# Queries of one chunk in a stage of their own instead of between attention's steps, and the order planned anew

## The chip, the cores and the metric

The kernel runs on one core of a Trainium2 chip. The core has engines that run their own instruction queues side by side: TensorE (PE in the profile; its weight loads are PEld), VectorE (DVE), ScalarE (ACT), GpSimd (POOL), and SyncE (SP), which here only issues DMA transfers. They meet through semaphores. SBUF is the on-chip memory, PSUM the eight banks that TensorE writes into.

The metric is the time of one execution on the device, in microseconds (us). Beside it there is a profiled execution, whose span is split up by engine, instruction and source line ("L640" is line 640 of the kernel before).

## The reference

Four blocks follow one another on x of 2048 tokens by 1024 features; each adds its result to x. Blocks 1 and 3 are a linear attention (A), blocks 2 and 4 softmax attention (B); A's and B's weights are used twice.

```python
def A(x, wqkv, w_phi, wo):
    q, k, v = ...                      # x @ wqkv, 32 heads of 32
    pq = q @ w_phi;  pk = k @ w_phi    # per head, 32 x 32
    phi_q = concat(softmax(pq), softmax(-pq))
    phi_k = concat(softmax(pk), softmax(-pk))
    kv = phi_k.T @ v;  z = sum(phi_k over tokens)
    o = (phi_q @ kv) / (phi_q @ z + 1e-6)
    return o @ wo

def B(x, wqkv, wo):
    q, k, v = ...
    p = softmax(q @ k.T * 32**-0.5)
    return (p @ v) @ wo

x = x + A(layernorm(x), ...);  x = x + B(layernorm(x), ...)
x = x + A(layernorm(x), ...);  x = x + B(layernorm(x), ...)
```

The text calls A the linear layer and B attention; so "the second linear layer" is the third block.

## The kernel before, in words

The tokens are four chunks (c = 0 to 3) of 512, each of four tiles of 128 rows. The features are eight groups (g) of 128, that is four heads each. x stays in SBUF (`xR`) for the whole kernel. All matrices are in bf16, sums in 32 bits.

**A linear layer** first makes keys and values of every chunk (`a_keys`), sums them up to a small state per head (`a_state`), and then makes, per chunk, the queries and with them the output (`a_queries`, `a_out`), the next row normalization (`ln_rows`), and the first keys and values for attention (`b_k`, `b_v`). For queries and keys the product of `wqkv` and `w_phi` is folded beforehand and lies in DRAM (`wd_q`, `wd_k`). `a_queries` treats half of a chunk's features at a time: four blocks of 128 features by 512 tokens, each made by eight matmuls (`mmg2`), then two exponentials on ScalarE (L1040), sums over heads, a weighting by the ratio of the two softmax sums, and numerator and denominator with the state.

**Attention** (`attention`) works through 32 turns, one for each chunk of queries and each group; a turn has 64 score blocks of 128 keys by 512 queries. A score block is one matmul (L1282). Two or three blocks lie in neighbouring PSUM banks and get one exponential on ScalarE (L1340). Other blocks are converted on VectorE instead (`convert`, L1438, one pass for a block; `exp_dve`, L1243 and L1248, four passes for a pair). Each block then goes into the products with values and with ones (L1481). Two sets of three PSUM banks hold scores, one bank the sums of L1481, and one bank, bank 7, is for "filling" work: the other keys, values and queries of attention, output projections of finished chunks, and, in the first attention, work of the second linear layer for chunks that are done. Filling work is made in 32-column form: four matmuls (L644) side by side for what elsewhere is one of 128 columns (L640). `mm` chooses the form.

In the first attention, when a chunk has its output, `ln_rows` normalizes it and `a_keys` makes its part of the keys' state (chunks 0, 1 and 2; the last chunk's follow in the linear layer's own stage). The normalized rows are kept in DRAM (`xd`, stored at L1719) and come back when queries are made (L1611).

For chunk 0 the kernel before goes a step further. `q_ahead` (L1011) loads chunk 0's rows again (L1724) and both halves of `wd_q` (L742), makes all eight blocks of queries in bank 7, copies each with VectorE to SBUF (L1022), and stores it to DRAM (`qf`, L1024). When the linear layer's stage begins, `a_queries` finds them in `q_saved`, loads them (L1036), and has no matmuls to do for them.

**What sets the order.** The kernel does not issue work in the order in which it is written. Every operation goes to a planner (`Sched`) with an engine, an expected duration, its predecessors, its buffers and a due time (`prio`); the planner plays through the engines' time and so fixes the order of each engine's queue, and where each buffer lies. Among its inputs are quotas on buffers of a kind (`QUOTA`; `MM_Q` is the number of PSUM banks that whole matmuls may hold, `MOST_E` that of exponentials waiting in attention), the due times of work (`PK` and `STEP`: row normalization and keys of chunks 0 to 2 in the first attention; `Q_LATE`: attention's queries of the late chunks; `OUT_AT`, `GO`, `PT`: output projections), and rules on when a score block goes to VectorE (`OPEN`, `NEAR`, `END`, `SLACK`). Where TensorE would have too little to do, the planner puts in filler matmuls whose results are not read (L1730 and L1734 with `onesD`, L1739 with `zero`).

The constant at the centre, and the two places that use it:

```python
QN = 1
...
            for c in range(QN, NC - 1):      # L1609: these chunks' rows come back for queries in the stage
                x_b, x_v = sb("xn", PO, C512)
...
            for c in range(QN):              # L1722: these chunks' queries are made in the first attention
                x_b, x_v = sb("xn1", PO, C512)
                q_ahead(c, at + QT[c], ...)
```

Of the kernel before, what the change touches and what calls it, by code (L numbers as in the profile page):

```python
# [61 lines left out]
class Sched:  # L62
# [139 lines left out]
    def run(self):  # L202
# [28 lines left out]
        while left:  # L231
# [173 lines left out]
RESERVE = 8 * 1024  # L405
LONG = {"kT", "v", "slab", "slabk", "xn", "xn1", "kvacc", "kvm", "zm", "wnat"}
MODEST = {"slabk", "xn1", "e1", "vp1", "pkf", "wo", "bo"}
MM_Q = 5
QUOTA = {"qf": 2, "qg": 6, "wqk": 1, "tl": 6, "pk": 6, "pv": 4, "kv": 3, "mm": MM_Q, "cmp": 3, "bc": 10, "num": 4, "wt": 4, "wx": 2, "fil": 5,
         "e": 6, "vp": 6, "e1": 4, "vp1": 4, "E": 10, "q2": 2, "kt": 4, "w2": 5, "oT": 26, "T": 4, "den": 2,  # L410
         "eq": 20, "ns": 12, "cw": 12, "hl": 6, "oc": 2, "slab": 8, "slabk": 3, "fin": 4,
# [10 lines left out]
QT = (184.5, 300, 310)  # L422
XQ = 5.39
QF_AT = 6.0
QN = 1
EVAC = (4, 4)
END = 28
FAR = (0, 0)
REST = 2.1
DIP = 4.0  # L430
# [19 lines left out]
HALF = (False, True)  # L450
VH = 3.38
V_LATE = (None, ((20.16, 6.58), (59.37, 7.17)))
Q_LATE = (lambda c, g: 104.52 + 4.56 * g if c == 2 else -5.67 + 18.61 * g, lambda c, g: 139.83 + 11.78 * g)
QL = (11, 9.91)
AW = 26
OUT_AT = (228.3, 245.85, 276.82)
GO = 2.98
BO = 296.78
PT = 3.56
QB = 18.16  # L460
PH = ((1, 22, 43), (1, 22, 43.51))
LA = 7.28
AHEAD_AT = 4
P0 = (133.6, 164.65, 226.59)
GAPS = (1.5, 2.78, 3.22)
PK = (142, 198.82, 255.37)
STEP = 3.45
AWAY = (-10, 12)
MIX = (lambda i: (1, 2, 1, 0)[i // 8], lambda i: (0, 0, 1, 0)[i // 8])
LOAD = (2.16, 2.38)  # L470
AHEAD = (25, 31)
SLACK = 4.16
THIRD_LOAD = (6.03, 1.29)
BOTH_LOAD = (0.97, 0.53)
EARLY = (80, 80)
# [3 lines left out]
XR = 40  # L479
SL = 30  # L480
HOLD = 0.81
OPEN = (0, 8)
MOST_E = (10, 15)
POOL = (0, 0)
BEHIND = (-3.39, 5.54)
NEAR = (10, 10)
LEAD = -1.02
MOST = (lambda i: 1 if i < 1 else 12, lambda i: 24 if i < 1 else 27)

# [18 lines left out]
def kernel(  # L508
# [746 lines left out]
    def attention(base, kT, vT, q_of, gate, most, mix, turns, pos, ahead, near, load, early, third_load, both_load, nb, opened, most_e, behind):  # L1255
# [114 lines left out]
        def lead():  # L1370
            return min(ahead, max(END, (len(units) - state["at"]) // 2))

# [11 lines left out]
        def wants(prio):  # L1384
# [4 lines left out]
            turn = pos[u[:2]]  # L1389
            if prio < prio_of(u) + SLACK:  # L1390
                return False
# [182 lines left out]
    for layer in range(2):  # L1574
# [31 lines left out]
        else:  # L1606
            wq_s = [slab("slab", second - SL + fc, wdq_v[:, :, fc * C512:(fc + 1) * C512], C512, [store["q"][fc]])
                    for fc in range(2)]
            for c in range(QN, NC - 1):  # L1609
                x_b, x_v = sb("xn", PO, C512)  # L1610
# [45 lines left out]
        for g in range(G):  # L1656
            pr = at + 10 * pos[(0, g)]
            w = slab("w2", pr - (QL[layer] + 3), B_w[:, :, g * P:(g + 1) * P], P) if g else wq0
            for qc in range(NC):
# [5 lines left out]
                else:  # L1665
                    pa = at + Q_LATE[layer](qc, g) if Q_LATE[layer](qc, g) is not None else pr + (AW if last else AWAY[qc - 2])
                    wa = w if pa < pr + 30 else slab("w2", pa - 3, B_w[:, :, g * P:(g + 1) * P], P)
# [6 lines left out]
        for qc, p0, gap in ((0, P0[0], GAPS[0]), (1, P0[1], GAPS[1]), (2, P0[2], GAPS[2])):  # L1674
            if last:
                p0, gap = OUT_AT[qc], GO
            for i in range(8):
# [13 lines left out]
        for i in range(G):  # L1691
            pr = p0 - 7 + PT * i
            t, fc = (i // 2, i % 2) if last else (i % 4, i // 4)
# [18 lines left out]
        if not last:  # L1712

            kv = new_kv()
            for c, p0 in ((0, PK[0]), (1, PK[1]), (2, PK[2])):
# [5 lines left out]
                    for i in range(4)]  # L1721
            for c in range(QN):  # L1722
                x_b, x_v = sb("xn1", PO, C512)
# [51 lines left out]
```

## Time and profile before

| | us |
|---|---|
| median of 3 runs | 2129.3 |
| lowest, highest | 2126.23, 2129.32 |
| profiled execution, its own time | 2128.77 |
| its span, first to last instruction | 2127.0 |
| first scores of the first attention start at | 309.4 |
| TensorE busy | 2074.9 |
| ScalarE busy | 1902.6 |
| VectorE busy | 1775.1 |

The span has five parts: loads and the first linear layer up to 309 us, the first attention up to about 1165, the second linear layer's stage up to about 1365, the second attention, and a short end. The rows are read as follows. A group has its line, engine and operation, what it writes and reads, how often it ran, then its busy time and the mean duration of one in ns, and last the idle time of the engine just before such instructions and what ended it. Durations of matmuls overlap, since they run in a pipeline: a matmul of 512 columns is listed with some 380 ns, while the next one starts after 0.22 us. A table by stretch gives, for the part of the span named first, its length and each engine's busy time in it, the granted TensorE clock as a share of full speed, the share of the DMA engines' time, and GB/s.

### The profile page before, as it was taken

The page shows a single profiled execution, that of the slowest core. Times are in us where ns is not written, and L with a number is a line of the kernel's source. Part 1 is how long each engine was busy: PE and PEld are TensorE (multiplying, and loading weights), DVE is VectorE, ACT ScalarE, POOL GpSimd, SP SyncE. Part 2 cuts the span into 40 slices and gives each one's busy share as a digit, 9 for nine tenths or more (in the row PEclk, how much of TensorE's full clock was granted, in tenths as well). Part 3 has the DMA queues.
Part 4 walks back from the last instruction along what each step waited for, and adds up shares of the span by engine and source line. Part 5 has one row for each costly group of instructions (what it writes and reads, how often), then busy time and mean ns, then how long its engine had stood idle before and what let it go on. Part 6 is the DMA issues. An engine that isn't in the chain of part 4 may idle for free.

```text
span 2127.0 us, 64995 instructions
## 1 busy us (share of the span) xinstructions
PE 2074.9 (98%) x27708; PEld 787.4 (37%) x27774; DVE 1775.1 (83%) x3310; ACT 1902.6 (89%) x2029; POOL 27.2 (1%) x83
## 2 busy tenths in 40 slices
PE   8999999999999999999999999999999999999999
PEld 5543443333333333333333434434333333333333
DVE  8866545757566899999999776798899999999998
ACT  7437769989999999999999577799999999999998
POOL 1000000000000000000000000000000000000000
PEclk9999999999999999999999999999999999999999
DMA  8730321121233322441355312211111122121111
GB/s 235 162 73 21 95 58 29 32 65 51 69 78 89 108 82 80 133 144 53 114 168 155 102 38 73 71 28 33 37 46 40 44 51 62 47 77 54 52 42 37
DMA packets 255467, 160.78 MB, mean 76 GB/s; under 512 B 147784, under 2 KB 229704, under 8 KB 255176
## 3 DMA queue, kind: packets, MB, share of 16 engines
q1 hardware_dynamic: 255176, 156.62, 27.2%
q8 instruction: 217, 3.56, 0.7%
q14 instruction: 74, 0.61, 0.1%
HBM read 89.72 MB, written 29.87 MB: 56 GB/s over the span
## 4 chain that ended last, share of the span: by engine, by line
PE 50%; ACT 26%; DVE 13%; issue 6%; DMA 4%; SPq 2%; ACTq 0%; DVEq 0%; POOL 0%; POOLq 0%
ACT arena L1340 23%; PE psum L640 15%; PE psum L644 13%; PE psum L1481 10%; PE psum L1282 9%; DVE arena L1438 4%; DVE work L1243 2%; DVE work L1248 2%; DVE arena L1248 2%; DMA arena<-rd 1%; PE psum L915 1%; DVE arena L1496 1%; SPq L731 1%; DMA arena<-in_A_wo_dram 1%; DMA arena<-arena 1%
## 5 line engine op out<-in xcount | busy, mean ns | idle before, releaser
L1340 ACT ACTIVATE arena<-psum 128x1536 bf16<-128x1536 f32 (+1 forms) x1332 | 1558.7, 1447 | 24.8 <-PE psum L1282 21.4
L644 PE MATMUL psum<-arena 128*32 128x512 bf16 (+1 forms) x9536 | 633.2, 365 | 9.2 <-DMA arena<-in_B_wqkv_dram 2.7
L1481 PE MATMUL psum<-arena 128*32 128x512 bf16 x4096 | 605.0, 383 | 1.3 <-DVE arena L1496 1.1
L1481 PE MATMUL psum<-arena,ones_bf 128*32 128x512 bf16 x4096 | 605.0, 383 | 0.0
L1282 PE MATMUL psum<-arena 32*128 32x512 bf16 x4096 | 523.9, 383 | 23.3 <-ACT arena L1340 16.5
L1438 DVE TENSOR_SCALAR arena<-psum 128x512 uint16<-128x512 f32 x663 | 446.4, 683 | 79.4 <-PE psum L1282 75.0
L640 PE MATMUL psum<-arena 128*128 128x512 bf16 (+1 forms) x1907 | 421.1, 372 | 7.8 <-issue 3.7
L1282 PEld LDWEIGHTS <-arena 32*128 32x128 bf16 x4096 | 160.0, 91 | 549.0 <-issue 545.5
L644 PEld LDWEIGHTS <-arena 128*32 128x32 bf16 x9536 | 209.1, 95 | 259.9 <-issue 162.2
L640 PEld LDWEIGHTS <-arena 128*128 128x128 bf16 x1968 | 185.7, 98 | 220.9 <-issue 21.4
L1243 DVE TENSOR_SCALAR work<-arena 128x1024 uint16<-128x1024 uint16 (+1 forms) x670 | 263.4, 415 | 2.3
L1481 PEld LDWEIGHTS <-arena 128*32 128x32 bf16 x4096 | 168.1, 95 | 211.8 <-issue 144.1
L1248 DVE TENSOR_TENSOR arena<-work 128x1024 bf16<-128x1024 bf16 x335 | 226.9, 677 | 2.6
L1248 DVE TENSOR_TENSOR work<-arena,work 128x1024 bf16<-128x1024 bf16 x335 | 226.5, 676 | 0.0
L1481 PEld LDWEIGHTS <-ones_bf 128*32 128x32 bf16 x4096 | 166.9, 95 | 22.3 <-issue 3.7
L880 ACT ACTIVATE arena<-psum 128x512 bf16<-128x512 f32 x80 | 43.7, 595 | 73.8 <-PE psum L640 67.8
L1145 DVE CAST arena<-psum 128x512 bf16<-128x512 f32 (+1 forms) x120 | 69.4, 579 | 42.7 <-PE psum L644 42.6
L1496 DVE COPY arena<-psum 128x512 f32<-128x512 f32 x126 | 86.0, 682 | 11.6 <-PE psum L1481 11.5
L884 DVE TENSOR_REDUCE arena<-arena 128x32 f32<-128x1024 bf16 x64 | 77.5, 1211 | 18.2 <-ACT arena L880 16.4
L1040 ACT ACTIVATE arena<-psum 128x512 bf16<-128x512 f32 x112 | 60.9, 616 | 25.7 <-PE psum L640 20.8
L893 DVE TENSOR_TENSOR arena<-psum,arena 128x1024 bf16<-128x1024 f32 x64 | 78.1, 1221 | 2.7
L685 ACT ACTIVATE arena<-xR 128x1024 bf16<-128x1024 bf16 x40 | 42.5, 1064 | 38.8 <-DVE xR L1119 38.8
(103 smaller groups left out, 994.1 us busy)
## 6 DMA issues: line engine op xcount, KB each, us to landing
arena<-in_B_wqkv_dram SPq DMA_DIRECT2D x66, 256.0 KB
arena<-rd SPq DMA_DIRECT2D x62, 256.0 KB
xa<-arena SPq DMA_DIRECT2D x48, 256.0 KB
arena<-in_A_wqkv_dram SPq DMA_DIRECT2D x40, 256.0 KB
arena<-in_B_wo_dram SPq DMA_DIRECT2D x40, 256.0 KB
arena<-arena SPq DMA_DIRECT2D x256, 32.0 KB
arena<-wd_k SPq DMA_DIRECT2D x32, 256.0 KB
arena<-arena SPq DMA_DIRECT2D x62, 128.0 KB
```

The costliest lines, as they stand in the source:

```text
L640: nc.tensor.matmul(out_, lhsT=lhsT, rhs=rhs, start=start, stop=stop, skip_group_check=True)
L644: nc.tensor.matmul(out_[ks, :], lhsT=lhsT[:, ks], rhs=rhs, start=start, stop=stop, tile_position=(0, 32 * k), skip_group_check=True)
L884: red = op("DVE", dve_us(1024) + 0.107, lambda ev=ev, sv=sv: nc.vector.reduce_sum(out=sv(), in_=ev().rearrange("p s (h d) -> p (s h) d", d ...
L893: ml = op("DVE", dve_us(1024), lambda vpv=vpv, wv_=wv_, sv=sv: nc.vector.tensor_tensor(out=wv_()[:, :, :, 0:DH], in0=vpv().rearrange("p (h ...
L1145: return soon(op("DVE", dve_us(n), lambda: nc.vector.tensor_copy(out=dst(), in_=src()), [dep], bufs, prio))
L1243: return sch.later("DVE", n * C512 / 3840 + 0.065, lambda: nc.vector.tensor_scalar(out=out_().bitcast(U16), in0=y_v().bitcast(U16), scalar ...
L1248: return sch.later("DVE", n * C512 / 1920 + 0.065, lambda: nc.vector.tensor_tensor(out=out_(), in0=in0(), in1=in1(), op=what), deps, [e_b, ...
L1282: nc.tensor.matmul(out=out_, lhsT=kT[g][1]()[r, pp, d * P:(d + 1) * P], rhs=q_of[(qc, g)][1]()[r, (pp + j // 2) % 2, :], start=True, stop= ...
L1340: ex = make("ACT", act_us(w * C512), lambda: nc.scalar.activation(out=e_v()[:, 0:w * C512], in_=s_v()[:, 0:w * C512], func=ACT.Exp, scale= ...
L1438: pair["got"].append(sch.later("DVE", dve_us(512), lambda: nc.vector.tensor_scalar(out=e_v().bitcast(U16)[:, k, :], in0=s_v(), scalar1=EXP ...
L1481: nc.tensor.matmul(out=a_v()[col:col + 32, :], lhsT=v_v()[:, kc % 4, o:o + DH] if what == 0 else ones_bf[:], rhs=ev()[:, x * C512:(x + 1) ...
L1496: cp = op("DVE", dve_us(512), lambda t_v=t_v, a_v=a_v: nc.vector.tensor_copy(out=t_v(), in_=a_v()), [last], [a_b, t_b], prio - 4)
```

## The change

`QN` goes from 1 to 0. So nothing is made ahead: `q_ahead` is no longer called, `q_saved` stays empty, chunk 0's rows are loaded from `xd` as those of chunks 1 and 2 are, and `a_queries` makes chunk 0's blocks with whole matmuls into PSUM and takes the exponentials from there. The other constants of the planner that differ are those of the diff.

```diff
-MM_Q = 5
+MM_Q = 4
...
-QN = 1
+QN = 0
...
-END = 28
+END = 26
...
-Q_LATE = (lambda c, g: 104.52 + 4.56 * g if c == 2 else -5.67 + 18.61 * g, lambda c, g: 139.83 + 11.78 * g)
+Q_LATE = (lambda c, g: 104.52 + 4.56 * g if c == 2 else -5.67 + 18.61 * g, lambda c, g: 139.83 + 11.25 * g)
...
-OUT_AT = (228.3, 245.85, 276.82)
-GO = 2.98
+OUT_AT = (228.3, 245.85, 276.27)
+GO = 2.92
...
-PT = 3.56
+PT = 3.17
...
-PK = (142, 198.82, 255.37)
-STEP = 3.45
+PK = (142, 190.15, 255.37)
+STEP = 3.35
...
-SLACK = 4.16
+SLACK = 3.94
...
-OPEN = (0, 8)
-MOST_E = (10, 15)
+OPEN = (0, 9)
+MOST_E = (11, 16)
...
-NEAR = (10, 10)
+NEAR = (8, 11)
```

A pair of values, as in `OPEN`, is for the first and the second attention; `Q_LATE`'s second function, `OUT_AT` and `GO` are for the second attention alone, `PK` and `STEP` for the first alone, and `MM_Q`, `END`, `PT` and `SLACK` for both.

## The prediction

> **What bounds the kernel now.** First the page's busy times and its chain of work that ended last.
>
> ```profile
> PE 2074.9 (98%) x27708; PEld 787.4 (37%) x27774; DVE 1775.1 (83%) x3310; ACT 1902.6 (89%) x2029; POOL 27.2 (1%) x83
> PE 50%; ACT 26%; DVE 13%; issue 6%; DMA 4%; SPq 2%; ACTq 0%; DVEq 0%; POOL 0%; POOLq 0%
> ```
>
> TensorE is nearly always busy and carries half of the chain, but ScalarE is at 89% too, so the average doesn't say which one a stage waits for. The table by stretch does: first layer's attention, the second linear layer's stage, second attention.
>
> ```profile
> 309.00:1165.00 856.00, 837.76 (x12296) 288.84 (x12298) 689.10 (x1251) 827.45 (x742) 10.27 (x24) 1.00 0.32 89
> 1165.00:1365.00 200.00, 193.75 (x1689) 89.09 (x1705) 139.57 (x262) 134.25 (x272) 2.82 (x8) 1.00 0.28 78
> 1365.00:2127.00 762.00, 743.67 (x10836) 263.34 (x10835) 728.73 (x1414) 750.94 (x651) 0.00 (x0) 1.00 0.18 46
> ```
>
> The columns after the length are PE, PEld, DVE, ACT, POOL, clock, DMA share, GB/s. In the linear stage TensorE alone is full (193.75 of 200 us); ScalarE has 66 us to spare. In attention two engines are full at once: 837.76 and 827.45 of 856, later 743.67 and 750.94 of 762. The change takes TensorE work out of the first kind of place, where TensorE shares the bound, and puts it into the second, where TensorE is the bound alone.
>
> The groups of the first attention's stretch say what is in TensorE's and ScalarE's time:
>
> ```profile
> L1340 ACT ACTIVATE arena<-psum 128x1536 bf16<-128x1536 f32 x403 | 601.1, 1611 | 17.2 <-PE psum L1282 14.6 <-PE psum L1481 1.6 <-PE psum L644 1.1
> L1340 ACT ACTIVATE arena<-psum 128x1024 bf16<-128x1024 f32 x277 | 314.4, 1178 | 6.2 <-PE psum L1282 5.5 <-PE psum L644 0.6
> L1438 DVE TENSOR_SCALAR arena<-psum 128x512 uint16<-128x512 f32 x284 | 192.3, 682 | 57.2 <-PE psum L1282 53.7 <-ACT arena L1340 2.2
> L1243 DVE TENSOR_SCALAR work<-arena 128x1024 uint16<-128x1024 uint16 x280 | 109.9, 420 | 1.8
> L1248 DVE TENSOR_TENSOR arena<-work 128x1024 bf16<-128x1024 bf16 x140 | 95.4, 681 | 1.5
> L644 PE MATMUL psum<-xR,onesD 128*32 128x512 bf16 x216 | 16.3, 381 | 0.8 <-DVE xR L1214 0.4 <-DVE arena L1438 0.2 <-DVE arena L876 0.2
> L1022 DVE COPY arena<-psum 128x512 f32<-128x512 f32 x8 | 5.5, 682 | 0.0
> ```
>
> ScalarE waits 23.4 us for TensorE in all (17.2 + 6.2), and TensorE fills 16.3 us with matmuls whose result nobody reads (x216 with `onesD`). So either engine has some 20 us of air in 856: neither can be shortened alone by much.
>
> **The change part by part. The matmuls taken out and put in.** `q_ahead` makes 8 blocks of 8 steps; each step is four 32-column matmuls (L644). In the linear stage the same 8 blocks are 64 whole matmuls (L640). Their prices, from the chain and from the timeline:
>
> ```profile
> 1187.08 10.74 PE psum L640 x49
> ```
>
> ```profile
> 1172.91 1.48 PE L644 MATMUL psum<-arena 128*32 128x512 bf16 x24
> ```
>
> A whole matmul advances by 10.74/49 = 0.219 us, so 64 cost 14.0 us. Six steps of four end after 1.48 us, of which about 0.38 is the last one's run-out: (1.48 - 0.38)/5 = 0.22 a step, 64 steps 14.1 us. TensorE's total does not change; 14 us change place.
>
> **What the linear stage pays.** At most 14.0 us. From that comes what the new matmuls can fill: places where TensorE stood, or ran a filler (L1734), while queries could have been made.
>
> ```profile
> 1166.97 0.82 PE L1734 MATMUL psum<-xR,onesD 128*128 128x512 bf16 x3
> ...
> 1182.52 1.89 PE L640 MATMUL psum<-arena 128*128 128x512 bf16 x8 [0.72 <-DMA arena<-xd]
> ```
>
> ```profile
> 1234.45 1.02 PE L1734 MATMUL psum<-xR,onesD 128*128 128x512 bf16 x3 [0.99 <-ACT arena L1057]
> ...
> 1236.57 0.39 PE L991 MATMUL psum<-arena,selr 32*128 32x512 bf16 x2 [0.78 <-DVE arena L1104]
> ...
> 1238.70 0.39 PE L640 MATMUL psum<-arena 128*128 128x512 bf16 x1 [0.21 <-DVE arena L1104]
> 1239.36 0.39 PE L991 MATMUL psum<-arena,selb 32*128 32x512 bf16 x2 [0.27 <-DVE arena L976]
> ```
>
> That is 3 x 0.22 + 0.72 at the start, and 0.99 + 0.78 + 0.21 + 0.27 + 3 x 0.22 around 1236: 1.4 + 2.9 = 4.3 us. The fillers after 1347 stand behind the last chunk's row normalization, where no queries are left. So the stage pays 9.7 to 14.0 us. I take 11.9, the middle: the first gap is filled only if the input is there, the second only if PSUM lets a later chunk's block wait, and the quota of "mm" banks falls from 5 to 4.
>
> **What the first attention gets back.** At least nothing: the work could have run in the air named above. At most 14.1 us, if TensorE alone sets the pace. The nearest rows are stretches of 20 us with little filling work (720 and 1040) against those in which `q_ahead` ran. Score matmuls (L1282), PE busy, clock, DMA:
>
> ```profile
> 720.00:740.00 20.00, 6.63 (x56) 2.10 (x56) 1.00 0.49 148
> 860.00:880.00 20.00, 5.87 (x45) 1.46 (x45) 1.00 0.59 188
> 880.00:900.00 20.00, 7.00 (x54) 2.19 (x54) 1.00 0.58 127
> 900.00:920.00 20.00, 6.73 (x54) 2.02 (x52) 1.00 0.56 170
> 1040.00:1060.00 20.00, 6.69 (x55) 2.35 (x55) 1.00 0.37 114
> ```
>
> And all engines in the same stretches:
>
> ```profile
> 720.00:740.00 20.00, 18.76 (x264) 6.41 (x257) 19.16 (x40) 20.00 (x19) 0.00 (x0) 1.00 0.49 148
> 860.00:880.00 20.00, 18.46 (x369) 6.57 (x365) 18.36 (x37) 18.60 (x18) 0.00 (x0) 1.00 0.59 188
> 880.00:900.00 20.00, 19.31 (x265) 6.24 (x258) 19.32 (x38) 20.00 (x19) 0.00 (x0) 1.00 0.58 127
> 900.00:920.00 20.00, 19.92 (x278) 6.34 (x276) 18.01 (x33) 20.00 (x19) 0.00 (x0) 1.00 0.56 170
> 1040.00:1060.00 20.00, 19.29 (x267) 6.63 (x260) 19.88 (x42) 20.00 (x20) 0.00 (x0) 1.00 0.37 114
> ```
>
> With the queries 45 + 54 + 54 = 153 scores in 60 us, 2.55 a us; without, 111 in 40 us, 2.78 a us. 153 scores at 2.78 take 55.1 us: 4.9 us less, a third of the 14.1. The reason is in the second fence: in the light stretches ScalarE is at 20.00 of 20 and VectorE at 19.16 and 19.88, so they set the pace as soon as TensorE doesn't. The 8 copies of L1022 (5.5 us of VectorE) lie in these stretches and are contained in the 4.9. I take 5.
>
> The Trainium skill says in "Perfetto Trace Analysis", section "Identifying the Most-Contended Engine", that one improves the engine with the highest occupancy, but that matmul busy time is no good measure for TensorE's. By its first half TensorE, whose work stays the same, would give a change of 0. The rows above, where a TensorE with 1.2 us of air in 20 went with a full ScalarE, agree with its second half; hence I price by scores per us.
>
> **The transfers.** Gone are 8 loads of `wd_q`, 4 of `xd` into the attention stage, 8 stores to and 8 loads from `qf`; 4 loads of `xd` for chunk 0 come in, ahead of the `wd_q` loads on SP's queue. At the boundary SP stood so:
>
> ```profile
> 1161.89 9.24 SPq L751 DMA_DIRECT2D arena<-in_A_wo_dram  x12
> 1171.18 4.82 SPq L1036 DMA_DIRECT2D arena<-qf  x4
> 1176.05 0.42 SPq L741 DMA_DIRECT2D arena<-in_B_wqkv_dram  x1
> 1176.57 2.03 SPq L1611 DMA_DIRECT2D arena<-xd  x4
> ```
>
> Chunk 1's `xd` loads, for which the matmul at 1182.52 waited 0.72 us, stood behind 4.82 us of `qf` loads, which go. I cost the transfers at 0: the 0.72 is counted already. If the cover goes, that is, if chunk 0's loads come as late as chunk 1's do here, TensorE has no query to make until some 11 us after 1171, which is a rival below.
>
> **The order planned anew** (`MM_Q`, `END`, `Q_LATE`, `OUT_AT`, `GO`, `PT`, `PK`, `STEP`, `SLACK`, `OPEN`, `MOST_E`, `NEAR`) adds no operation. `PK` and `STEP` move chunk 1's keys forward into the place the queries leave, which is how the 5 us can be had at all. The others move due times and how early score blocks go to VectorE. One block moved from ScalarE to VectorE saves ScalarE 1.611 - 1.178 = 0.43 us and costs VectorE 0.682 + 0.42 + 0.68 = 1.78 us (half of each of the pair's four passes besides the first). First attention has 856 - 689 = 167 us of free VectorE time; 20 more blocks, 36 us of it, would be worth 8.7 us, and 20 fewer cost as much, against 284 now. So its bounds are -8.7 and +8.7; I take 0, since no row tells the sign. In second attention VectorE is busy 728.73 of 762 and there is less room than that.
>
> **Sum.** The profiled execution took 2128.77 us with a span of 2127.0, 0.5 below the median of 2129.3. 2128.8 + 11.9 - 5 + 0 = 2135.7; about 2135.5 as a median is within what the terms can carry. A measurement of this kernel tells about 0.2%, 4.3 us, from no change; +6.4 us is 0.3%.
>
> **The rivals.** *TensorE's freed time is used in full (faster).* The first attention gives back 14 us and the linear stage pays only 9.7; that alone is -4.4. Beside it the new order puts 10 more blocks on VectorE (-4.3): about 2120. For it speaks the 23.4 us in which ScalarE waited for TensorE, and VectorE's 57.2 us of waiting at L1438; against it, that VectorE is full just where the queries ran. It decides from the point where more than some 12 us come out of the first attention.
>
> *The two places cancel (same).* TensorE sets the pace in both, 14 out and 14 in: 2129. The 98% speak for it, the light stretches against it.
>
> *Chunk 0's input comes late (slower still).* If its `xd` loads stand behind L751 as chunk 1's did, nothing fills TensorE from 1171 on for up to 11 us; part of that is covered by chunk 3's keys. 2128.8 + 14 - 5 + 5 = 2143. Against it: their due time lies 10 before that of the `wd_q` loads.
>
> *The clock.* Less work in attention could let the granted clock fall:
>
> ```profile
> 2060.00:2080.00 20.00, 17.42 (x198) 5.41 (x195) 19.90 (x40) 19.98 (x17) 0.00 (x0) 0.86 0.12 32
> ```
>
> Here it did, to 0.86, a loss of about 2.8 us of full clock, with TensorE busy 17.42 us of 20. At 720 and 1040 the fillers held it at 1.00, so one such stretch more or less is worth at most 3 us and decides nothing alone. The Trainium skill ("TensorE: Matmul & The Clock Gate", "What's actually happening") lets the clock halve after an idle window of about 3.4 us; by that no stretch of attention would be at risk, which this row doesn't bear out.
>
> **How the numbers follow.** My sum, with its own range of 2129 to 2143 (9.7 - 10 at one end, 14.0 - 0 at the other): 0.45, of which 0.38 is slower by over 0.2% and 0.07 within. TensorE's time used in full: 0.34, of which 0.32 faster, 0.02 within. Cancelling: 0.14, of which 0.08 within and 0.03 to either side. Late input: 0.07, of which 0.05 slower, 0.01 within, 0.01 faster. Together faster 0.36, same 0.18, slower 0.46. The range for 8 in 10 reaches from the full-use rival's side, 2118, to the late input's, 2145.
>
> **What would show it.** Right: the linear stage, from the last score of the first attention to the first of the second (195 us here), grows by 10 to 14 us, with about 64 more L640 matmuls in it, and the first attention shrinks by some 5 us with ScalarE still full. Wrong: first attention shorter by over 10 us, with more than 284 L1438 there (VectorE took over blocks), or a linear stage that grew by less than 9 us (gaps I didn't count were filled), or any change beyond 4 us in the first linear stage or second attention, where my sum has 0.

## The result and the profile after

The changed kernel is slower by a little: 2132.06 us against 2128.07 us (medians of 17 runs each). The ratio is 1.0016 with a 95% interval of 1.0009 to 1.0023, that is +3.4 us (1.9 to 4.9). The forecast was 2135.5, slower by 0.3%. The sign was right and the time lies in the stated range. But the difference is below the 0.2% that the prediction took for the least that a measurement can tell, so by its own classes this is "the same", to which it gave 0.18. And the two terms of the sum were both wrong, by 8.6 and 5 us in opposite directions, as the stages show.

The page of the changed kernel, busy times and chain:

```profile
PE 2073.0 (97%) x27630; PEld 789.4 (37%) x27697; DVE 1774.8 (83%) x3313; ACT 1901.4 (89%) x2025; POOL 25.5 (1%) x83
PE 50%; ACT 31%; DVE 9%; issue 6%; DMA 3%; SPq 2%; ACTq 0%; DVEq 0%; POOL 0%; POOLq 0%
```

To compare stages, one set of borders serves for all kernels: the first attention goes from its first score (L1282) to the end of its last product with values (L1481), the linear stage from there to the first score of the second attention. The table by stretch with these borders, first the changed kernel (first attention, linear stage, rest):

```profile
312.00:1168.60 856.60, 831.93 (x12181) 287.62 (x12186) 688.69 (x1256) 826.34 (x738) 8.88 (x24) 1.00 0.31 85
1168.60:1365.90 197.30, 194.94 (x1628) 91.50 (x1641) 134.70 (x250) 129.64 (x265) 2.58 (x8) 1.00 0.24 66
1365.90:2131.90 766.00, 745.38 (x10930) 263.88 (x10930) 733.91 (x1422) 755.25 (x655) 0.00 (x0) 1.00 0.17 45
```

and the kernel before with the same borders:

```profile
309.40:1166.00 856.60, 838.32 (x12304) 289.21 (x12306) 689.13 (x1251) 828.25 (x743) 10.27 (x24) 1.00 0.32 89
1166.00:1360.00 194.00, 188.07 (x1612) 87.41 (x1635) 135.04 (x252) 128.35 (x264) 2.82 (x8) 1.00 0.28 79
1360.00:2127.00 767.00, 748.39 (x10893) 264.64 (x10894) 733.22 (x1422) 755.83 (x656) 0.00 (x0) 1.00 0.18 46
```

The first attention takes 856.6 us in both. It gave nothing back, though TensorE is busy there 6.4 us less. One execution is uncertain here by some 2 us: in that of the changed kernel TensorE had half its clock for 3.4 us of this attention (from 1134.9 us on), in that of the kernel before for none of it. Three more executions below have the order of the changed kernel's first attention (in one of them up to its last 25 us), each with a fall of the clock too; all four lie between 855.2 and 858.0 us, and none shows the 5 us that were forecast. The linear stage grew by 3.3 us, the rest shrank by 1. The profiled executions (2133.7 and 2128.77 us) also differ by 2.6 us before the first score, where the program is the same: TensorE's granted clock was 0.89 over the first 30 us there, 0.94 before.

What happened in the first attention is in its groups, of the changed kernel:

```profile
L1340 ACT ACTIVATE arena<-psum 128x1536 bf16<-128x1536 f32 x405 | 603.0, 1620 | 17.1 <-PE psum L1282 15.2 <-PE psum L1481 1.9
L1340 ACT ACTIVATE arena<-psum 128x1024 bf16<-128x1024 f32 x273 | 309.6, 1178 | 6.8 <-PE psum L1282 6.5 <-PE psum L644 0.3
L1438 DVE TENSOR_SCALAR arena<-psum 128x512 uint16<-128x512 f32 x287 | 194.5, 683 | 57.2 <-PE psum L1282 53.3 <-ACT arena L1340 2.3 <-issue 0.2
L644 PE MATMUL psum<-xR,onesD 128*32 128x512 bf16 x280 | 22.1, 382 | 2.7 <-issue 1.7 <-DVE xR L1214 0.6 <-DVE arena L1438 0.4
```

ScalarE and VectorE do what they did (403 + 277 exponentials and 284 conversions before). In the place of the queries' 14.1 us stand more fillers (280 instead of 216, and 96 instead of 72 of L1739: 22 steps or 4.8 us) and some 2.8 us of output work that the kernel before left to the next stage. The rest is the 6.4 us by which TensorE is less busy.

And in the linear stage, first the changed kernel, then the kernel before (L644 are partial output projections of the first attention's last chunk that were not done in time; L1734 fillers):

```profile
L640 PE MATMUL psum<-arena 128*128 128x512 bf16 x670 | 153.8, 379 | 2.0 <-issue 1.3
L644 PE MATMUL psum<-arena 128*32 128x512 bf16 x48 | 2.9, 380 | 0.0
L1734 PE MATMUL psum<-xR,onesD 128*128 128x512 bf16 x10 | 2.8, 379 | 0.1
```

```profile
L640 PE MATMUL psum<-arena 128*128 128x512 bf16 x611 | 141.4, 379 | 3.3 <-issue 1.6 <-DMA arena<-xd 0.7 <-DVE arena L1104 0.2
L644 PE MATMUL psum<-arena 128*32 128x512 bf16 x88 | 5.7, 381 | 0.0
L1734 PE MATMUL psum<-xR,onesD 128*128 128x512 bf16 x17 | 5.0, 379 | 1.3 <-ACT arena L1057 1.0 <-issue 0.2
```

The queries are there: 62 more weight loads of L640 in the stage (822 instead of 760), and two before its border. Weight loads are counted here, since some records of matmuls are missing in the traces. Taking for each TensorE instruction the time to the next one's start, L640 costs 11.3 us more, L644 2.75 us less, the fillers 1.9 less, L991 and L1051 2.3 less, and the others 1.0 less: together +3.3. Since 62 matmuls at 0.219 us are 13.6 us, the waits behind L640 have become shorter by 2.3 us.

### The profile page after: what moved, and what is told of

Same layout as the page of the kernel before. It is cut to its first block, busy times and chain, and to the rows that moved or that the text cites. A ratio compares the mean times of both kernels' runs of the same rounds, so it can differ in the third digit from the quotient of the medians.

```text
span 2131.9 us, 64788 instructions
## 1 busy us (share of the span) xinstructions
PE 2073.0 (97%) x27630; PEld 789.4 (37%) x27697; DVE 1774.8 (83%) x3313; ACT 1901.4 (89%) x2025; POOL 25.5 (1%) x83
## 4 chain that ended last, share of the span: by engine, by line
PE 50%; ACT 31%; DVE 9%; issue 6%; DMA 3%; SPq 2%; ACTq 0%; DVEq 0%; POOL 0%; POOLq 0%
ACT arena L1340 30%; PE psum L640 18%; PE psum L644 12%; PE psum L1481 9%; PE psum L1282 9%; DVE arena L1438 2%; DVE work L1243 1%; DVE arena L1248 1%; DVE work L1248 1%; PE psum L915 1%; SPq L731 1%; DMA arena<-arena 1%; DMA arena<-in_B_wqkv_dram 1%; ACT arena L880 0%; PE psum L991 0%
## 5 line engine op out<-in xcount | busy, mean ns | idle before, releaser
L644 PE MATMUL psum<-arena 128*32 128x512 bf16 (+1 forms) x9280 | 614.8, 365 | 8.0 <-DVE arena L876 2.6
L1481 PE MATMUL psum<-arena 128*32 128x512 bf16 x4096 | 605.2, 382 | 1.2 <-DVE arena L1496 0.6
L1481 PE MATMUL psum<-arena,ones_bf 128*32 128x512 bf16 x4096 | 604.9, 382 | 0.6 <-issue 0.6
L1282 PE MATMUL psum<-arena 32*128 32x512 bf16 x4096 | 521.0, 383 | 30.1 <-ACT arena L1340 23.2
L640 PE MATMUL psum<-arena 128*128 128x512 bf16 (+1 forms) x1967 | 434.8, 373 | 9.1 <-issue 3.3
L1282 PEld LDWEIGHTS <-arena 32*128 32x128 bf16 x4096 | 160.6, 91 | 554.7 <-issue 550.9
L644 PEld LDWEIGHTS <-arena 128*32 128x32 bf16 x9280 | 203.3, 95 | 247.8 <-issue 151.6
L640 PEld LDWEIGHTS <-arena 128*128 128x128 bf16 x2032 | 192.2, 98 | 229.0 <-issue 21.9
L1481 PEld LDWEIGHTS <-arena 128*32 128x32 bf16 x4096 | 166.9, 95 | 213.0 <-issue 147.1
L1248 DVE TENSOR_TENSOR arena<-work 128x1024 bf16<-128x1024 bf16 (+1 forms) x337 | 227.7, 676 | 2.3
L1248 DVE TENSOR_TENSOR work<-arena,work 128x1024 bf16<-128x1024 bf16 (+1 forms) x337 | 227.7, 676 | 0.0
L1481 PEld LDWEIGHTS <-ones_bf 128*32 128x32 bf16 x4096 | 165.4, 95 | 21.1 <-issue 2.9
L880 ACT ACTIVATE arena<-psum 128x512 bf16<-128x512 f32 x80 | 43.7, 595 | 75.6 <-PE psum L640 69.6
L1145 DVE CAST arena<-psum 128x512 bf16<-128x512 f32 (+1 forms) x120 | 69.4, 578 | 42.1 <-PE psum L644 41.9
L1040 ACT ACTIVATE arena<-psum 128x512 bf16<-128x512 f32 x128 | 69.7, 622 | 26.9 <-PE psum L640 22.0
```

Source lines behind the costliest of these rows:

```text
L640: nc.tensor.matmul(out_, lhsT=lhsT, rhs=rhs, start=start, stop=stop, skip_group_check=True)
L644: nc.tensor.matmul(out_[ks, :], lhsT=lhsT[:, ks], rhs=rhs, start=start, stop=stop, tile_position=(0, 32 * k), skip_group_check=True)
L1040: ex = [op("ACT", act_us(512), lambda s=s, pv=pv, ev=ev: nc.scalar.activation(out=ev()[:, s, :], in_=pv(), func=ACT.Exp, scale=(1.0, -1.0) ...
L1248: return sch.later("DVE", n * C512 / 1920 + 0.065, lambda: nc.vector.tensor_tensor(out=out_(), in0=in0(), in1=in1(), op=what), deps, [e_b, ...
L1282: nc.tensor.matmul(out=out_, lhsT=kT[g][1]()[r, pp, d * P:(d + 1) * P], rhs=q_of[(qc, g)][1]()[r, (pp + j // 2) % 2, :], start=True, stop= ...
L1481: nc.tensor.matmul(out=a_v()[col:col + 32, :], lhsT=v_v()[:, kc % 4, o:o + DH] if what == 0 else ones_bf[:], rhs=ev()[:, x * C512:(x + 1) ...
```

## The experiments

Four questions: which part does what (the constant or the order), what TensorE's work costs in each place, which engine sets the pace there, and which constant of the order it is. Unless the text says otherwise, "stage" is the linear stage with the borders above, and totals are ratios to the kernel before on the same chip.

The stages of the profiled executions, all in us:

```
                                first attention   linear stage   partial outputs left    total, ratio (95%)
before                              856.6            194.1         88 L644
changed kernel                      856.7            197.3         48                    1.0016 (1.0009 to 1.0023)
QN = 0 alone                        861.8            203.9        120                    1.0060 (1.0047 to 1.0072)
new constants, QN = 1               858.6            217.2        224                    1.0098 (1.0084 to 1.0112)
before, q_ahead cut                 862.0            194.0         88                    1.0027 (1.0017 to 1.0037)
before, q_ahead doubled             868.8            194.2         88                    1.0050 (1.0037 to 1.0062)
before, 8 exponentials doubled      869.4            193.2         88                    1.0054 (1.0041 to 1.0067)
before, 8 copies doubled            865.2            193.2         88                    1.0015 (1.0006 to 1.0023)
before, 18 exponentials cut         859.4            194.2         88                    0.9994 (0.9985 to 1.0003)
before, both cuts                   860.1            193.6         88                    1.0013 (1.0004 to 1.0022)
changed, own queries cut            857.1            196.8         48                    1.0020 (1.0010 to 1.0030)
changed, own queries doubled        858.0            210.7         48                    1.0070 (1.0058 to 1.0082)
changed, PT old                     855.2            197.3         48                    1.0014 (1.0005 to 1.0022)
changed, PK and STEP old            857.7            203.5        120                    1.0052 (1.0040 to 1.0064)
```

**The constant alone.**

```diff
-QN = 1
+QN = 0
```

> The kernel before with QN = 0 alone; all other constants stay. The planner lays the order out again for the lighter first attention, but with the old due times. Theory A (TensorE's work between attention's steps lay in its air, the linear stage is paced by TensorE): the linear stage, from the last L1481 of the first attention to the first score of the second, grows by 14.0 us less what gaps and fillers swallow (5.3 us in the changed kernel), about +8.7 us; the first attention changes by less than 2 us; in all +6 to +10 us against before. The new constants would then be worth some 5 us of the way back to the +3.4 us measured for the whole change. Rival B (the first attention does give time back, and the new constants lose it again): here the first attention is 4 to 10 us shorter and the total lies between -2 and +4 us.

Measured: +0.60%, 12.8 us, more than theory A's +6 to +10. The stage grew by 9.8 us, as theory A had it, and the first attention did not shrink either: it grew by 5.2 us, where theory A allowed 2; some 4 us of that were lost at two places, near 610 and 760 us, where the granted clock was at half for 3.4 us each. Rival B, an attention that gives back 4 to 10 us, is refuted. The new constants win back 9 of the 12.8 us.

**The new constants alone.**

```diff
 # the changed kernel
-QN = 0
+QN = 1
```

> The changed kernel with QN = 1: the new constants alone, queries of chunk 0 again between attention's steps. Theory A: the linear stage falls back by about 8 us from the changed kernel's 197.3 us, the first attention stays at 857 us within 3 us; total 5 us below the changed kernel, that is -2 us against before. Rival B (constants planned for QN = 0 only fit QN = 0, since PK puts chunk 1's keys where the queries go): the first attention grows by over 4 us and the total is +2 us or more against before.

Measured: +0.98%, 21 us, which theory A missed by far. Rival B's bound for the total (+2 us or more) holds, but not its place: the attention grew by 2 us, the stage by 23. The stage's groups say why:

```profile
L644 PE MATMUL psum<-arena 128*32 128x512 bf16 x224 | 14.3, 381 | 3.3 <-issue 1.9 <-DVE arena L1214 1.3
L1734 PE MATMUL psum<-xR,onesD 128*128 128x512 bf16 x54 | 13.7, 380 | 0.6 <-ACT arena L1099 0.6
```

With the queries in bank 7 again and chunk 1's keys pulled forward, everything behind them in that bank came later. 224 instead of 88 matmuls of the partial outputs were left when attention ended, chunk 3's row normalization waited for them, and TensorE ran 54 fillers. So the new constants are good only with the constant `QN = 0`.

**Less of the work in attention, with the order untouched.** Here and in the next five runs the planner sees the kernel it knows, so each engine's order stays as it is and only instructions are left out or issued twice.

```diff
-    def mmg2(pb, pv, lhs, rhs, d1, d2, bufs, prio, lo=0, hi=4, more=False, share=1.0):
+    def mmg2(pb, pv, lhs, rhs, d1, d2, bufs, prio, lo=0, hi=4, more=False, share=1.0, emit=tuple(range(8)), again=0):
...
-                for po in range(at, at + step):
+                for po in [p for p in range(at, at + step) if p in emit for _ in range(1 + again)]:
...
-                         fin, wd, [xb, wb, f_b], pr)
+                         fin, wd, [xb, wb, f_b], pr, emit=(0, 7))
```

> The kernel before, the same order on every engine, but q_ahead issues only 2 of the 8 steps of each block: 48 of 64 steps (10.6 us of TensorE at 0.22 us) are left out between attention's steps, and nothing is moved or replaced; chunk 0's queries of the second linear layer are so the sum of 2 of 8 partial products. Theory A (air): 0 to -1 us. My prediction's price (a third): -3.7 us. TensorE alone paces attention: -10.6 us.

Measured: not shorter, but +0.27%. Neither the third of my prediction nor the full price holds. The +0.27% itself goes with a lower clock: over the 8 runs the mean granted clock was 0.9952, over the 16 of the kernel before on the same chip 0.9978. That is 5.5 us of full clock in 2130, and the means of the times differ by 5.4 us. (Of the 5.4 us by which the first attention is longer in the profiled execution, 2.2 came near 610 us, ahead of the cut, in a low clock; the rest is taken up below.)

**More of it.**

```diff
-                         fin, wd, [xb, wb, f_b], pr)
+                         fin, wd, [xb, wb, f_b], pr, again=1)
```

> The kernel before, the same order, but every step of q_ahead is issued twice: 64 more steps, 14.1 us of TensorE, between attention's steps (chunk 0's queries come out with seven of eight partial products doubled). Theory A (air): the added work first fills idle time, then costs; the two ends are 0 and +14.1 us, and with some 1 us of air in each 20 us of that stretch (45 us long) I expect +8 to +12 us, much more than the cut gave back. A straight price of a third: +5 us. TensorE alone paces attention: +14 us and -10.6 us for the cut.

Measured: +0.50%, 10.6 us; in the profiled execution the first attention grew by 12.2 us for 14.1 us of work. So the price has a corner just where the kernel before stands: adding costs most of it, taking away brings nothing.

**ScalarE and VectorE in the same stretch.**

```diff
-            ex = make("ACT", act_us(w * C512), lambda: nc.scalar.activation(
-                out=e_v()[:, 0:w * C512], in_=s_v()[:, 0:w * C512], func=ACT.Exp, scale=e_scale),
+            ex = make("ACT", act_us(w * C512), lambda: [nc.scalar.activation(
+                out=e_v()[:, 0:w * C512], in_=s_v()[:, 0:w * C512], func=ACT.Exp, scale=e_scale) for _ in range(1 + (base < 500 and n in range(444, 476, 4)))],
```

> The kernel before, the same order, but 8 of ScalarE's exponentials in the stretch of the first attention in which q_ahead runs are issued twice: about 8 x 1.17 = 9.4 us more on ScalarE, none on TensorE. Theory A (ScalarE paces that stretch): +7 to +9.4 us. If TensorE paces it: +0 to +4 us.

```diff
-                cp = soon(op("DVE", dve_us(512), lambda pv=pv, f_v=f_v: nc.vector.tensor_copy(out=f_v(), in_=pv()),
+                cp = soon(op("DVE", dve_us(512), lambda pv=pv, f_v=f_v: [nc.vector.tensor_copy(out=f_v(), in_=pv()) for _ in range(2)],
```

> The kernel before, the same order, but each of the 8 copies of q_ahead's blocks from PSUM (L1022) is issued twice: 5.5 us more on VectorE in the stretch where q_ahead runs. If VectorE paces that stretch beside ScalarE, +3 to +5.5 us, and the change's taking the copies out was worth about as much; if VectorE has slack there, under +1.5 us.

Measured: +0.54% (11.5 us) for ScalarE, +0.15% (3.2 us) for VectorE's 5.5 us. Then ScalarE's exponentials are cut, alone and together with the cut of `q_ahead` (its edit joined to this one):

```diff
-                out=e_v()[:, 0:w * C512], in_=s_v()[:, 0:w * C512], func=ACT.Exp, scale=e_scale),
+                func=ACT.Exp, scale=e_scale, **{k: v()[:, 0:w * C512].rearrange("p (a b) -> p a b", a=w)[:, :, 0:256 if base < 500 and n in range(444, 480, 2) else C512] for k, v in (("out", e_v), ("in_", s_v))}),
```

> The kernel before, the same order, but 18 of ScalarE's exponentials in the stretch of the first attention where q_ahead runs take only 256 of the 512 columns of each score block (the other columns keep what the buffer held before): 0.64 or 0.43 us off each, about 10 us off ScalarE. Theory C (corner: TensorE, ScalarE and VectorE are equally full there, so that adding to any one costs nearly all of it and taking from one alone brings next to nothing): 0 to -2 us, just as the cut of TensorE's 10.6 us brought nothing. If ScalarE alone paces the stretch: -8 to -10 us.

> The kernel before, the same order, with both cuts at once: 48 of 64 steps of q_ahead left out (10.6 us of TensorE) and the 18 exponentials taken over half the columns (about 10 us of ScalarE). Theory C: with two of the three engines relieved the stretch shortens by clearly more than either cut alone, -3 to -8 us, VectorE with its 1 us of air in 20 setting the rest. If neither engine has anything to do with that stretch's pace (transfers, or the order itself): within 2 us of before, like each cut alone.

Measured: 0.9994 with ScalarE's 10 us cut, no gain, as theory C said; with both cuts 1.0013, some 2 to 3 us more, which theory C did not say. On its face that is the other case on record, within about 2 us of before: that neither engine has to do with the pace. The clock speaks against taking it so. With both cuts its mean over the 12 runs was 0.9955, in the kernel before 0.9977, which is 4.7 us of full clock; counted in full, the kernel with both cuts would be 2.7 us faster than before. With the exponentials cut alone the clock was as before (0.9980).

The seven kernels can be laid beside one another in one stretch, from the 1320th to the 1500th score of the first attention, which holds all of `q_ahead`; each row is the table by stretch of that kernel (length; PE, PEld, DVE, ACT, POOL; clock). In order: before; q_ahead cut; ScalarE cut; both cut; q_ahead doubled; ScalarE doubled; copies doubled.

```profile
863.70:935.70 72.00, 69.43 (x955) 22.66 (x951) 67.51 (x127) 70.60 (x67) 0.65 (x2) 1.00 0.57 165
```

```profile
865.80:938.80 73.00, 61.03 (x763) 19.84 (x759) 67.49 (x127) 70.81 (x67) 0.65 (x2) 0.98 0.54 162
```

```profile
868.00:940.90 72.90, 69.42 (x955) 21.98 (x951) 66.83 (x126) 62.76 (x67) 0.66 (x2) 1.00 0.57 163
```

```profile
864.50:937.50 73.00, 65.57 (x760) 19.57 (x757) 67.39 (x127) 60.93 (x67) 0.65 (x2) 0.91 0.56 163
```

```profile
863.30:947.60 84.30, 82.51 (x1208) 28.20 (x1205) 68.72 (x126) 73.01 (x67) 0.66 (x2) 1.00 0.49 141
```

```profile
864.90:948.80 83.90, 71.46 (x952) 23.31 (x949) 68.58 (x127) 82.04 (x75) 0.65 (x2) 0.98 0.48 142
```

```profile
867.20:945.00 77.80, 71.25 (x952) 22.14 (x951) 72.10 (x134) 71.71 (x67) 0.65 (x2) 0.98 0.52 153
```

Before, three engines are nearly full at once: 69.4, 67.5 and 70.6 of 72 us. With TensorE relieved (61.0), ScalarE holds the length (70.8 of 73.0); with ScalarE relieved (62.8), TensorE does (69.4 of 72.9). The waits in these stretches show the same: what waited, for what, then us, times and the longest. Before, TensorE and ScalarE hardly wait for each other:

```profile
PE psum L1282 <- ACT arena L1340: 0.7, 2, 0.5
ACT arena L1340 <- PE psum L1282: 1.4, 1, 1.4
```

With `q_ahead` cut TensorE waits for ScalarE, and with the exponentials cut ScalarE for TensorE:

```profile
PE psum L1282 <- ACT arena L1340: 9.1, 22, 0.9
```

```profile
ACT arena L1340 <- PE psum L1282: 6.6, 17, 1.2
ACT arena L1340 <- PE psum L1481: 2.7, 3, 1.8
```

Lengthening any one of the three lengthens the stretch: by 12.3 us for TensorE's 14.1, by 11.9 for the 11.4 us that the doubled exponentials really took, by 5.8 where VectorE's busy time rose by 4.6 (with the clock low for 3.4 us in each of the last two). With both relieved, TensorE is nevertheless busy 65.6 us, although 10.6 us of its work are gone: its granted clock was at half three times in this stretch, for 13.7 us in all, a mean of 0.91. That took up to 6.8 us of what the cuts gave, and VectorE was at 67.4 of 73.0. ScalarE waited there 11.7 us for TensorE, and TensorE now waited for VectorE:

```profile
ACT arena L1340 <- PE psum L1282: 8.1, 10, 1.6
ACT arena L1340 <- PE psum L1481: 3.6, 3, 1.7
PE psum L1282 <- DVE arena L1438: 2.3, 4, 0.8
PE psum L1481 <- DVE arena L1496: 1.3, 3, 0.8
```

How much of the 73 us is the clock's and how much VectorE's was not tried apart; it stays open. So does what the two kernels with less of `q_ahead` lost at two places further on (2.7 and 2.4 us; in the first kernel near 1088 and 1116 us), where nothing was left out and no low clock is on record; the kernel with the exponentials cut lost nothing there. Even with the lost clock and these two places counted in full, leaving out 10.6 us of `q_ahead` is worth some 5.5 + 2.7 - 5.4 = 2.8 us at most.

**Less and more of it in the linear stage.**

```diff
 # the changed kernel, with mmg2 as above
-                     fin, qd, [xb, qb], prio)
+                     fin, qd, [xb, qb], prio, emit=(0, 7) if c == 0 and len(wq_s[hf]) == 3 else tuple(range(8)))
```

> The changed kernel, the same order on every engine, but of chunk 0's query blocks in the second linear layer only 2 of 8 steps are issued: 48 whole matmuls (10.5 us at 0.219 us) are left out in the linear stage; chunk 0's queries are the sum of 2 of 8 partial products. If TensorE alone paces the stage: -10.5 us against the changed kernel, -7 us against before. If the stage has another chain close behind (exponentials, row normalization, transfers), so that the last of these matmuls came nearly for nothing: -3 to -6 us against the changed kernel, about 0 to -2 us against before, with TensorE's gaps of 0.2 us and more coming back in the stage.

```diff
 # the changed kernel, with mmg2 as above
-                     fin, qd, [xb, qb], prio)
+                     fin, qd, [xb, qb], prio, again=c == 0 and len(wq_s[hf]) == 3)
```

> The changed kernel, the same order, but every matmul of chunk 0's query blocks in the second linear layer is issued twice: 64 more, 14.0 us (the values come out wrong in the same way as in the doubled q_ahead). The changed kernel has no gap of 0.2 us or more left on TensorE in the stage, so every theory expects nearly the full price here: +12 to +14 us against the changed kernel, +15 to +17 us against before. Less than +9 us would say that another chain than TensorE's sets the stage's length.

Measured: the cut brings nothing (1.0020, the changed kernel 1.0016; the stage 196.8 instead of 197.3), the doubling costs 13.4 us of stage for 14.0. The cut was expected to give back at least 3 us, and neither of its two cases came true. Other engines' work stood close behind. The groups of the cut kernel's stage show the new waits:

```profile
L716 PE MATMUL psum<-ident,arena 128*128 128x128 bf16 x64 | 4.7, 219 | 1.2 <-DVE arena L706 1.2
L991 PE MATMUL psum<-arena,selb 32*128 32x512 bf16 x32 | 4.6, 392 | 2.7 <-DVE arena L976 2.6
L915 PE MATMUL psum<-arena 128*32 128x33 bf16 x256 | 2.4, 184 | 1.6 <-DVE arena L893 1.6
```

These 5.5 us are waits for VectorE's part of the row normalization, the softmax ratio and the keys' state; in the changed kernel the same groups had none. Waits of L640 add 1.4 us, half of them for ScalarE's L721, and the clock was at half for 3.4 us near 1216, which is up to 1.7 us. These account for most of the 10.5 us, not all. So the linear stage has the same corner as the first attention.

**Which constant wins the time back.**

```diff
 # the changed kernel
-PT = 3.17
+PT = 3.56
```

> The changed kernel with PT back at 3.56: the partial output projections of the last chunk keep their old due times, all else stays. The order differs only from the end of the first attention on. If PT is what moved these partial products (18 steps of L644, 4.2 us, between the first run and the changed kernel) out of the linear stage: the stage, 197.3 us in the changed kernel, is 2 to 5 us longer, total +5 to +8 us against before. If PT is idle here: +3.4 us, as the changed kernel.

```diff
 # the changed kernel
-PK = (142, 190.15, 255.37)
-STEP = 3.35
+PK = (142, 198.82, 255.37)
+STEP = 3.45
```

> The changed kernel with PK's second value and STEP back at 198.82 and 3.45: chunk 1's keys in the first attention keep their old due times and leave a hole where the queries were. If these constants close the hole: the first attention is 3 to 5 us longer (861.8 us with all old constants, 856.7 us in the changed kernel), total +6 to +9 us against before. If the hole costs nothing: +3.4 us, as the changed kernel.

Measured: `PT` does nothing (1.0014; the stage to a tenth the same). `PK` and `STEP` are worth 0.36%, 7.6 us, but not where I expected it: the attention is only 1 us longer without them, the stage 6.3 us. Its groups:

```profile
L640 PE MATMUL psum<-arena 128*128 128x512 bf16 x671 | 154.7, 379 | 2.7 <-issue 1.4 <-ACT arena L1087 0.3
L644 PE MATMUL psum<-arena 128*32 128x512 bf16 x120 | 7.4, 380 | 0.0
```

120 instead of 48 partial outputs are left over, 4.5 us. They go through bank 7, as the keys do. The last copy of the keys out of that bank (L876) starts, in the changed kernel, in the kernel before, and with the old `PK` and `STEP`, at

```profile
L876 DVE COPY arena<-psum x24: 675/682/693, 751.7 to 1119.8; 128x512 f32<-128x512 f32 x24
```

```profile
L876 DVE COPY arena<-psum x24: 674/681/692, 749.8 to 1133.0; 128x512 f32<-128x512 f32 x24
```

```profile
L876 DVE COPY arena<-psum x24: 679/684/716, 753.4 to 1140.9; 128x512 f32<-128x512 f32 x24
```

that is 1119.8, 1133.0 and 1140.9 us (1148.7 with `QN = 0` alone, 1163.5 with the new constants and `QN = 1`). With 48, 88, 120, 120 and 224 matmuls left, in all five kernels a later end of the keys goes with as many or more left over. That the one makes the other is argued from the one bank that both pass through; no run moved the keys' end alone. Why the keys end later with `QN = 0` alone than before, though the queries are gone from the bank, is open.

## Why the prediction was right, and where it was not

*What bounds the kernel.* That TensorE shares the bound in attention and carries the linear stage was right for added work, in both places (doubling costs 12.3 of 14.1 and 13.4 of 14.0 us in the profiled stages, 10.6 and 11.5 in the totals). It was wrong for work taken away: VectorE, which I left out of the bound in the first attention for its 689 of 856 us, is as full as the others in the stretch that matters (67.5 of 72), and in the linear stage VectorE's chains follow close behind a TensorE that looked alone. The Trainium skill's rule of one most-contended engine ("Perfetto Trace Analysis", "Identifying the Most-Contended Engine") doesn't fit such a stretch: with 69.4, 67.5 and 70.6 us busy of 72, relieving TensorE or ScalarE by some 10 us changed nothing.

*What the linear stage pays* (11.9): measured +3.3. The new matmuls are 13.6 us by themselves, as I had it. The gaps and fillers that I counted at up to 4.3 us and took half of gave 7.5: 1.9 of fillers, 2.3 at L991 and L1051, 2.3 behind L640 and 1.0 of small ones. What is missing in the sum is that 40 matmuls of partial outputs, 2.75 us, left the stage; I had no row on them. So my sign of being wrong, a stage that grew by less than 9 us, did come, and uncounted gaps are only a part of its reason. With the old order the stage grew by 9.8 us, the lower end of my 9.7 to 14.0, with 32 more matmuls of partial outputs in it.

*What the first attention gets back* (5): measured 0. This is the step that failed. I read 4.9 us from stretches with little filling work, but those stretches also differ in what else the planner put there; a slope between stretches of different mix is not the price of taking one job out. Of the 4.9 us, 3.8 came from one row, 860 to 880 us with 45 scores. The first copy of a query block ran only at 873.4 us, and that row also holds 128 matmuls of the keys' state:

```profile
L1022 DVE COPY arena<-psum x8: 679/682/684, 873.4 to 913.9; 128x512 f32<-128x512 f32 x8
```

```profile
L915 PE MATMUL psum<-arena 128*32 128x33 bf16 x128 | 1.3, 182 | 0.0
```

In the two other rows with queries, 880 to 920 us, there are 108 scores, which at 2.775 a us take 38.9 us: 1.1 us less, not 4.9. Cut alone, the job gives nothing back (first attention 862.0 instead of 856.6 us in a profiled execution, 1.0027 in total, with the lower clock told above), and in the changed kernel fillers, partial outputs and air stand in its place.

*The transfers* (0): right. Chunk 0's `xd` loads were issued between 1124.4 and 1127.1 us, 40 us ahead of use, the 0.7 us wait is gone, and the rival of a late input did not come.

*The order planned anew* (0, between -8.7 and +8.7): it is worth some -9 us beside the constant, just outside my bound, and by another mechanism. I bounded score blocks that change engine; they hardly did (287 conversions for 284). What went with the gain is the queue for bank 7: with `PK` and `STEP` pulled forward into the time that the queries left in it, the keys end 13 us earlier, and 40 more matmuls of partial outputs are done before attention ends. Either one alone leaves more over: 120 matmuls with `QN = 0` alone, 224 with the new constants alone. The attention's freed time came back as work taken over from the next stage, not as a shorter attention. One constant pair, `PK` and `STEP`, carries most of it (7.6 us); `PT` has no part, nor has `MM_Q`, with whose old value every engine's program is the same. The other constants were not tried one by one.

*The rivals.* Full use of TensorE's freed time: refuted by the cut. Cancelling: the nearest in its time, though its reason (TensorE's pace in both places) fell with the cuts. The clock: at half for 3.4 or 6.8 us, up to four times in an execution after its first 30 us, each worth at most 3.4 us, as I had it. That it decides nothing held between the two kernels, but not in the runs with `q_ahead` cut, where some 5 us go with it. So that the sum came out near the time is in part luck, because its misses partly cancel: 8.6 us too much in the stage, 5 us too much given back in attention, and 1 us less in the rest, which I had at 0.

## What to carry to other kernels

In a kernel whose order was planned until several engines are full together, a job can have two prices, as here: nearly its full length where it is put, and little or nothing where it is taken from; so moving work costs, unless something else moves into the hole. Where work passes through one narrow place (here one PSUM bank), look at what stands behind it in that queue and where that ends, not at the stage from which the job was taken. Issue the job twice or cut it, with the order untouched, to get both prices before believing a slope between stretches of a profile. And look at the granted clock of every run: a cut can lose to the clock what it saves.

## What the runs showed of the hardware that was not expected

The granted clock falls to half for 3.4 or 6.8 us at a time, 27 times in the 14 profiled executions after their first 30 us. The same place can have such a fall in one execution and not in another. The table by stretch around 610 us, in the kernel before, with q_ahead cut, and with the exponentials cut; all three have the same program there:

```profile
600.00:620.00 20.00, 17.70 (x257) 5.75 (x258) 9.77 (x19) 18.20 (x15) 0.00 (x0) 1.00 0.35 84
```

```profile
600.00:620.00 20.00, 17.11 (x223) 5.22 (x220) 8.45 (x17) 16.33 (x14) 0.00 (x0) 0.91 0.33 77
```

```profile
600.00:620.00 20.00, 17.79 (x234) 5.40 (x230) 9.00 (x18) 17.12 (x14) 0.00 (x0) 0.91 0.37 87
```

The first kept its clock at 1.00, the others had it at half for 3.4 us, and fell behind by 2.2 and 1.4 us between the 660th and the 720th score. But the place is no accident: in all 14 executions TensorE stands there for 1.7 to 3.0 us until filling work is released (mostly L644, waiting for a load of attention's weights). Nine of them fell to half clock between 608 and 612 us, five did not. Here are the 3.4 us before the fall in the kernel with q_ahead cut, the 3.3 us after it, and a stretch of 3.4 us at the same stop in the kernel before, where no fall followed:

```profile
606.90:610.30 3.40, 1.52 (x20) 0.42 (x20) 0.69 (x1) 1.01 (x2) 0.00 (x0) 1.00 0.27 61
610.40:613.70 3.30, 3.30 (x31) 0.92 (x31) 0.00 (x0) 2.26 (x3) 0.00 (x0) 0.50 0.75 162
```

```profile
606.70:610.10 3.40, 1.89 (x26) 0.65 (x30) 0.79 (x2) 1.60 (x2) 0.00 (x0) 1.00 0.32 71
```

In the 3.4 us before each of the 27 falls TensorE was busy 0.8 to 2.4 us. So it was never idle for the whole of it, but it had always stood for 1 us or more in all. The reverse does not hold: stretches with as little as 1.6 us passed without a fall. The Trainium skill ("TensorE: Matmul & The Clock Gate", "What's actually happening") names an idle window of about 3.4 us as the condition and calls the window free-running; the second agrees with a fall that comes at the same stop in nine executions and not in five, and within each execution the changes of the clock lie whole multiples of 3.41 us apart; if idle means without any matmul, the first does not agree with these rows. It also means that taking TensorE work away can slow TensorE: with both cuts the stretch from 864.5 to 937.5 us ran at 0.91, where the kernel before had 1.00, and over all timed runs both kernels with less of `q_ahead` had a lower mean clock (0.9952 and 0.9955 against 0.9978 and 0.9977), while the one with the exponentials cut had not.
